# Normalised tokens turned by DRAM and VectorE instead of TensorE, in the MLP half of an adaLN block (pairs 1 to 7)

## The chip, the cores and the metric

One core of a Trainium2 chip. The metric is device time in microseconds (us) of one execution of the whole kernel. The engines are called by their names in the profile: PE (TensorE matmuls, with PEld for its weight loads), DVE (VectorE), ACT (ScalarE), POOL (GpSimd) and SP (SyncE, which here only issues DMAs). All data is float32; matmuls run on float32r operands, each split into a high and a low part and multiplied in three terms.

## The reference

An adaptive-layernorm transformer block: an attention half and then an MLP half. S = 2048 tokens, D = 640 features, F = 1728 hidden features. The half that matters here:

```python
mod = (_silu(c) @ w_mod).reshape(c.shape[0], 6, 1, -1)
sa, ca, ga, sb, cb, gb = (mod[:, 0], mod[:, 1], mod[:, 2], mod[:, 3], mod[:, 4], mod[:, 5])
...
x = x + ga * _A_ref(h, A_wqkv, A_w_phi, A_wo)
h = _layernorm(x, axis=-1) * (1 + cb) + sb
x = x + gb * _B_ref(h, B_w1, B_b1, B_w2, B_b2)
# _B_ref: h = relu(x @ w1 + b1) ** 2 ; out = h @ w2 + b2
```

## The kernel before

**Tiles.** The 2048 tokens are 8 pairs of 2 x 128 tokens (`NB` = 8 pairs, j = 0 to 7). The 640 features are `NC` = 5 chunks of 128, the hidden features 14 blocks (`NF`, the last one 64 wide) taken two at a time: `NP` = 7 double blocks, n = 0 to 6.

**A step.** The MLP runs pair by pair; each pair takes 14 steps, and in step `at` = 2n or 2n + 1 PE does `up(j, at)`, which multiplies chunk by chunk W1's block with the pair's normalised and transposed tokens `H2[j]` (15 matmuls of 256 columns: five chunks, three terms each, 10 in step 13), and then `down(0)` or `down(1)`, one half of W2's product for the double block before. What `up` leaves in PSUM goes ACT relu (L1255), DVE square (L1256), then ACT copy to the high part `ra` (L1279) and DVE subtraction to the low part (L88); pairs from `PLAIN` = 2 on also form four sums on DVE (L1270) and split those into `rs` (L1295 on ACT, L88 on DVE). `down` multiplies `ra` and `rs` with W2's rows, which lie in SBUF or, from pair 2 on, come from DRAM through a ring of four buffers (`ring_a`, `ring_b`, `ring_c`, issued by POOL).

**The next pair's input.** While pair j runs, `layer(j + 1, at)` does the work for the next pair, by a table per pair (`LN_AT0` for pair 1, `LN_AT1` for 2, `LN_AT2` for 3, `LN_AT` for 4 to 7) that names the step of each piece: "load" and "xx" fetch attention's result `XM` and the residual `XX`, "add" adds them on DVE (L1079) and stores the sum, "ln" gives the steps of six ACT passes (two sums L1503, two sums of squares L1508, two scalings L1515, one for each tile of 128 tokens; small POOL instructions L1505 and L1510 to L1512 stand between them), and the entries with a number call `t2` for the chunks named. `t2` transposes two tiles of one or two chunks on PE (`t_in`, L357, a matmul with the identity, into a PSUM bank) and turns them into `H2` (`t_out`: ACT scale and shift L368 with the condition's columns `cols_b`, ACT copy to the high part L369, DVE subtraction to the low part L88). `XX` serves as scratch for `t_out`. Pair 0's input is made in the attention half.

**What sets the order.** In the MLP the order on PE, DVE, ACT and POOL is the order in which the code emits the instructions (`manual_schedule`), and SP's too, but for pair 1, where a scheduler places its DMAs. Each engine works its own list in order, so an instruction that waits holds all that stand behind it. On ACT and DVE a step's own work stands first, and `layer`'s pieces of that step behind it.

Of the kernel before, what the change touches and what calls it, by code (L numbers as in the profile page):

```python
# [8 lines left out]
F32 = mybir.dt.float32  # L9
# [12 lines left out]
NT = S // P  # L22
NC = D // P
# [28 lines left out]
def kernel(  # L52
# [19 lines left out]
    nc = tc.nc  # L72
# [14 lines left out]
    def lo(out_lo, full, hi, eng=None):  # L87
        (eng or nc.vector).tensor_tensor(out_lo, full, hi.bitcast(F32), op=ALU.subtract)  # L88
# [8 lines left out]
    dram = ctx.enter_context(tc.tile_pool(name="dram", bufs=1, space=bass.MemoryType.DRAM))  # L97
# [19 lines left out]
    def row(tag, name):  # L117
        return (pc if tag in ("s3", "s4") else mem).tile([P, D], F32, tag=tag, name=name, bufs=BUFS[tag])
# [19 lines left out]
    def tp(name):  # L138
        return psA.tile([P, 512], F32, tag="tp", name=name)
# [20 lines left out]
    ident = const.tile([P, P], F32, name="ident")  # L160
# [10 lines left out]
    cols_b = const.tile([P, 10], F32, name="cols_b")  # L171
# [145 lines left out]
    MA = {}  # L317
# [34 lines left out]
        for _ in ln_parts(xt, nm, spare):  # L352
            pass

    def t_in(xn, d, p):
        for i in range(2):
            nc.tensor.transpose(p[:, i * P : (i + 1) * P], xn[:, i, d * P : (d + 1) * P], ident)  # L357

    def t_unit(xn, cols, hT, d, nm, p=None):
        if p is None:  # L360
            p = tp(f"t{nm}_{d}")
        t_in(xn, d, p)
        t_out(cols, hT, d, nm, p)

    def t_out(cols, hT, d, nm, p, hf=None):
        if hf is None:
            hf = row("s3", f"hf{nm}_{d}")[:, :256]
        nc.scalar.activation(hf, p[:, :256], AF.Identity, bias=cols[:, d : d + 1], scale=cols[:, 5 + d : 6 + d])  # L368
        nc.scalar.activation(hT[:, d, 0], hf, AF.Copy)  # L369
        lo(hT[:, d, 1], hf, hT[:, d, 0])  # L370
# [12 lines left out]
    def t1(j, *ds, more=None):  # L383
        if 0 in ds:
            HT[j] = ht(f"hT{j}", j)
        p = tp(f"ta{j}_{ds[0]}")
        for k, d in enumerate(ds):
            t_in(XB[j], d, p[:, 256 * k : 256 * k + 256])
        if more:
            mod_turn(more[0], p[:, 256:], 4)  # L390
        for k, d in enumerate(ds):
            t_out(cols_a, HT[j], d, f"a{j}", p[:, 256 * k : 256 * k + 256])
        DONE[:] = newest(ET_.Activation), newest(ET_.DVE)
        if more:
# [318 lines left out]
    for t in range(2, NT - 2):  # L713
        j, i = divmod(t, 2)
# [12 lines left out]
        p = proj("v", t, (1, 0, lambda: t1(j + 1, 4)) if t == NT - 3 else None)  # L727
# [76 lines left out]
    def bank(nm):  # L804
        return psB.tile([P, 512], F32, tag="m", name=nm)
# [226 lines left out]
    todo = {"load": list(preps), "hi": list(preps), "lo": list(preps)}  # L1032
# [29 lines left out]
    def load_xm(j):  # L1062
        XM[j] = tok2("x0", f"xm{j}")
        for i in range(2):
            nc.sync.dma_start(XM[j][:, i], A1[2 * j + i])

    def load_xx(j):
        if j:
            XX[j] = [row("s2" if j <= PLAIN else "s1", f"xx{j}_{i}") for i in range(2)]
        else:  # L1070
            both = tok2("x1", "xx0")
            XX[j] = [both[:, i] for i in range(2)]
        for i in range(2):
            t = 2 * j + i
            nc.sync.dma_start(XX[j][i], x[t * P : (t + 1) * P])
# [6 lines left out]
    def t2(j, *ds):  # L1082
        if 0 in ds:
            H2[j] = ht(f"h2_{j}", j, (0, 96))
        if j == 0:
            t_unit(XM[j], cols_b, H2[j], ds[0], f"b{j}", bank(f"tb{j}_{ds[0]}"))
            return
        p = tp(f"tb{j}_{ds[0]}")
        for k, d in enumerate(ds):
            t_in(XM[j], d, p[:, 256 * k : 256 * k + 256])  # L1090
        for k, d in enumerate(ds):
            t_out(cols_b, H2[j], d, f"b{j}", p[:, 256 * k : 256 * k + 256], XX[j][d % 2][:, :256])

    NB = NT // 2
    places += [new(f"w{w}") for w in W_AT[-23:-19] + W_AT[-18:-16] + W_AT[-15:]] + [new(tag) for tag in ("k", "k", "q0", "q1")]
# [393 lines left out]
    prev = None  # L1489
    LN2 = {}  # L1490

    LN_AT0 = {"load": 2, "xx": 3, "add": (5, 6), "ln": (5, 6, 7, 7, 8, 9), 10: (0, 1), 11: (2, 3), 12: (4,)}
    LN_AT1 = {"load": 3, "add": (5, 5), "ln": (5, 6, 6, 7, 8, 8), 9: (0, 1), 11: (2, 3), 12: (4,)}
    LN_AT2 = {"load": 0, "xx": 3, "add": (6, 6), "ln": (7, 7, 8, 8, 9, 9), 10: (0, 1), 11: (2, 3), 12: (4,)}
    LN_AT = {"load": 0, "add": (3, 4), "ln": (4, 5, 6, 6, 7, 7), 8: (0, 1), 10: (2, 3), 12: (4,)}
    PREPS = iter([1, 3] + [2, 1, 2, 2, 1, 2] + [1, 1] + [1, 2])

    def ln_pieces(xt, nm, spare):
# [204 lines left out]
```

## Time and profile before

| what | value |
|---|---|
| median of 3 runs (lowest, highest) | 766.42 us (765.6, 767.21) |
| the profiled execution's own time | 766.05 us |
| its span, first to last instruction | 764.3 us |
| busy: PE / DVE / ACT / POOL | 758.5 / 593.9 / 435.6 / 144.9 us |
| granted TensorE clock | 1.000 |
| DMA moved | 126.69 MB, mean 166 GB/s |
| MLP half | from 387.7 us to the end; a pair takes about 46 us |

A time in the traces counts from the span's start. A row of a timeline gives start, length, engine, line, operation, output and inputs, and how many instructions were merged; in brackets stands how long the engine sat idle before and who released it. Instructions on an engine overlap a little, so the pace is read from start to start.

### The profile page before, as it was taken

How to read it: one execution, taken by the hardware profiler on the slowest of the kernel's cores; microseconds unless marked ns; L12 is line 12 of the kernel's file. 1: busy time of each engine (PE TensorE's matmuls, PEld its weight loads, DVE VectorE, ACT ScalarE, POOL GpSimd, SP SyncE). 2: the span in 40 equal slices, each digit the busy share in tenths (PEclk: the TensorE clock that was granted, in tenths of full speed). 3: DMA queues.
4: the chain of work that ended last, by engine and by line, in shares of the span. 5: the costliest groups of instructions: out<-in, count | busy, mean ns of one | idle time of the engine just before them, and what ended most of it. 6: DMA issues, size and time to landing. Idle time of an engine off the chain costs nothing.

```text
span 764.3 us, 15303 instructions
## 1 busy us (share of the span) xinstructions
PE 758.5 (99%) x5968; PEld 739.7 (97%) x5968; DVE 593.9 (78%) x1083; ACT 435.6 (57%) x972; POOL 144.9 (19%) x301
## 2 busy tenths in 40 slices
PE   9999999999999999999999999999999999999997
PEld 8999999999999989988999999999999999999997
DVE  6598897988999899999655667876767666685666
ACT  5766756677853364546776647465563645536331
POOL 3001101001100255432101000231321313213110
PEclk9999999999999999999999999999999999999999
DMA  8811431343332345223366466996766759767460
GB/s 322 329 61 78 138 104 54 104 136 112 126 104 93 109 150 188 72 87 104 122 194 221 120 227 236 283 334 209 224 166 207 232 179 268 199 184 204 126 184 35
DMA packets 51505, 126.69 MB, mean 166 GB/s; under 512 B 6684, under 2 KB 7457, under 8 KB 51433
## 3 DMA queue, kind: packets, MB, share of 16 engines
q1 hardware_dynamic: 34098, 84.65, 32.8%
q0 software_dynamic: 14752, 35.76, 16.9%
q10 hardware_dynamic: 2583, 5.30, 1.8%
q8 instruction: 47, 0.77, 0.5%
q14 instruction: 25, 0.20, 0.1%
HBM read 95.70 MB, written 29.89 MB: 164 GB/s over the span
## 4 chain that ended last, share of the span: by engine, by line
PE 91%; DVE 7%; DMA 1%; issue 0%; SPq 0%; ACT 0%; DVEq 0%
PE up L78 24%; PE acc L78 18%; PE pq L78 9%; PE pk L78 9%; PE pv L78 9%; PE pwo L78 6%; PE acc3x L78 5%; PE kvp L450 3%; PE te L920 1%; DVE dn L878 1%; DVE scr L876 1%; DVE ezb L900 1%; PE tb L357 1%; PE ta L357 1%; DVE ot L88 1%; PE foldq L280 1%
## 5 line engine op out<-in xcount | busy, mean ns | idle before, releaser
L78 PE MATMUL up<-h,w 128*128 128x256 f32 x1640 | 206.4, 278 | 0.0
L78 PEld LDWEIGHTS up<-h,w 128*128 128x128 f32 x1640 | 196.1, 188 | 0.0
L1255 ACT ACTIVATE ft<-up,b_t 128x256 f32<-128x256 f32 x104 | 49.1, 472 | 113.8 <-PE up L78 113.2
L78 PE MATMUL acc<-w,ra 128*128 128x384 f32 x452 | 97.4, 335 | 0.0
L1256 DVE TENSOR_TENSOR ft<-ft 128x256 f32<-128x256 f32 x104 | 44.1, 424 | 48.4 <-ACT ft L1255 46.8
L78 PE MATMUL pwo<-wo,ot 128*128 128x256 f32 (+3 forms) x512 | 80.5, 312 | 0.1
L78 PEld LDWEIGHTS pwo<-wo,ot 128*128 128x128 f32 (+1 forms) x512 | 74.4, 188 | 3.2 <-issue 2.7
L78 PE MATMUL pq<-wq,hT 128*128 128x384 f32 (+1 forms) x480 | 75.2, 312 | 0.0
L78 PEld LDWEIGHTS acc<-w,ra 128*128 128x128 f32 x452 | 72.7, 188 | 0.8 <-DVE ra L88 0.5
L78 PE MATMUL pk<-wk,hT 128*128 128x384 f32 (+1 forms) x480 | 72.7, 308 | 0.0
L78 PE MATMUL pv<-wv,hT 128*128 128x384 f32 (+1 forms) x480 | 71.7, 307 | 0.0
L78 PEld LDWEIGHTS pq<-wq,hT 128*128 128x128 f32 x480 | 71.1, 188 | 0.6 <-issue 0.2
L78 PEld LDWEIGHTS pk<-wk,hT 128*128 128x128 f32 x480 | 70.5, 188 | 0.4 <-issue 0.2
L78 PEld LDWEIGHTS pv<-wv,hT 128*128 128x128 f32 x480 | 70.1, 188 | 0.0
L88 DVE TENSOR_TENSOR ra<-ft,ra 128x384 fp32r<-128x384 f32 (+2 forms) x86 | 36.8, 449 | 32.6 <-ACT ra L1279 19.3
L1365 POOL DMA_DIRECT2D ring_a<-td_a x34 | 18.3, 539 | 126.1 <-PE acc L78 100.4
L1279 ACT ACTIVATE ra<-ft 128x384 fp32r<-128x384 f32 x48 | 25.2, 526 | 28.4 <-DVE ft L1256 22.4
L78 PE MATMUL acc3x<-w,ra 128*128 128x256 f32 x231 | 39.8, 278 | 0.0
L78 PEld LDWEIGHTS acc3x<-w,ra 128*128 128x128 f32 x231 | 37.2, 188 | 0.2 <-DVE ra L88 0.2
L1270 DVE TENSOR_TENSOR ft<-ft 128x128 f32<-128x128 f32 x136 | 33.4, 287 | 1.2
L441 DVE TENSOR_REDUCE sk<-ek 128x64 f32<-128x1280 f32 x16 | 23.7, 1484 | 12.4 <-ACT ek L436 10.8
L884 POOL TENSOR_TENSOR dn<-dn,rs_q 128x32 f32<-128x32 f32 x32 | 20.2, 630 | 66.7 <-DVE dn L878 66.4
(270 smaller groups left out, 1412.6 us busy)
## 6 DMA issues: line engine op xcount, KB each, us to landing
ring_c<-td_c POOLq DMA_DIRECT2D x34, 384.0 KB, 4.2
ring_a<-td_a POOLq DMA_DIRECT2D x34, 384.0 KB, 4.1
ring_b<-td_b POOLq DMA_DIRECT2D x34, 256.0 KB, 4.0
esp<-eq SPq DMA_DIRECT2D x12, 640.0 KB, 3.0
el<-esp SPq DMA_DIRECT2D x12, 640.0 KB, 3.9
rw<-in_w SPq DMA_DIRECT2D x23, 320.0 KB, 2.9
wm<-in_w_mod SPq DMA_DIRECT2D x20, 320.0 KB, 3.3
xb<-in_x SPq DMA_DIRECT2D x8, 640.0 KB, 4.2
```

The costliest lines, as they stand in the source:

```text
L78: nc.tensor.matmul(o, a, b, start=first and i == 0, stop=last and i == len(terms) - 1, skip_group_check=skip,)
L88: (eng or nc.vector).tensor_tensor(out_lo, full, hi.bitcast(F32), op=ALU.subtract)
L280: nc.tensor.matmul(p[g // 3][:, (g % 3) * 120 : (g % 3) * 120 + n], r, bd_t[:120, g * 120 : g * 120 + n], start=True, stop=True,)
L357: nc.tensor.transpose(p[:, i * P : (i + 1) * P], xn[:, i, d * P : (d + 1) * P], ident)
L441: nc.vector.tensor_reduce(s, heads(flat(e)), axis=AX.X, op=ALU.add)
L450: nc.tensor.matmul(kvp[g // 4][64 * c : 64 * c + 64, a : a + 2 * n].rearrange("p (s n) -> p s n", s=2), v[:, u], e[:, :, o : o + n], start ...
L884: nc.gpsimd.tensor_tensor(dn[:, s], dn[:, s], rs[:, 1 - s], op=ALU.mult)
L1255: nc.scalar.activation(r, p, AF.Relu, bias=b1_t[:, f : f + 1])
L1256: nc.vector.tensor_tensor(r, r, r, op=ALU.mult)
L1270: nc.vector.tensor_tensor(t[:, o], t[:, a], t[:, b], op=op)
L1279: nc.scalar.activation(a[:, 0, :3], t[:, :3], AF.Copy)
L1365: nc.gpsimd.dma_start(RING[j, n, r], TD[n][r].bitcast(F32R))
```

## The change

For pairs 1 to 7 the PE transposes are taken out. In their place, after a pair's second scaling, `deal(j)` writes the normalised tokens with four DMAs to a DRAM buffer `XN`, one DMA for each 32 partitions, and `dealt(j)` reads them back with two DMAs into `XX`, so that partition 32q + t then holds, of the tokens 32a + t, the q-th quarter of the features. `turn(j)` transposes blocks of 32 x 32 on DVE (two instructions, one for each tile, each of 640 columns) from `XX` into `XM`. Feature 5p + b then lies on partition p in chunk b; W1's rows (on the host) and the condition's shift and scale columns (`mod_turn` for parts 3 and 4) are put in the same order, and pair 0's PE transposes read their columns with a step of five. `t_out` takes its input from `XM` in SBUF and writes its scaled result in place. `XM` thus stays in use until the last `t_out`. The tables move: the six ACT passes come earlier or closer together, `turn` is in step 10, `dealt` in step 9, and `t_out` in steps 11, 12 and 13 (chunks 0 and 1, 2 and 3, and 4).

```diff
@@ mod_turn
-            nc.tensor.transpose(p[:, i * P : (i + 1) * P], MA[part][:, c * P : (c + 1) * P], ident)
+            src = by_turn(MA[part])[:, c] if part in (3, 4) else MA[part][:, c * P : (c + 1) * P]
+            nc.tensor.transpose(p[:, i * P : (i + 1) * P], src, ident)
...
+    def by_turn(ap):
+        return ap.rearrange("p (f b) -> p b f", b=NC)
@@ t2
-        p = tp(f"tb{j}_{ds[0]}")
-        for k, d in enumerate(ds):
-            t_in(XM[j], d, p[:, 256 * k : 256 * k + 256])
-        for k, d in enumerate(ds):
-            t_out(cols_b, H2[j], d, f"b{j}", p[:, 256 * k : 256 * k + 256], XX[j][d % 2][:, :256])
+        for d in ds:
+            hf = XM[j].rearrange("p s d -> p (s d)")[:, 256 * d : 256 * d + 256]
+            t_out(cols_b, H2[j], d, f"b{j}", hf, hf)
+
+    XN = [dram.tile([4, 2, P, D // 4], F32, name=f"xn{j}") for j in range(NT // 2)]
+
+    def deal(j):
+        for a in range(4):
+            nc.sync.dma_start(
+                XN[j][a].rearrange("i (q t) c -> t i q c", q=4),
+                XM[j][32 * a : 32 * a + 32].rearrange("t i (q c) -> t i q c", q=4),
+            )
+
+    def dealt(j):
+        for i in range(2):
+            nc.sync.dma_start(XX[j][i].rearrange("p (a c) -> p a c", a=4), XN[j][:, i].rearrange("a p c -> p a c"))
+
+    def turn(j):
+        xt = XM[j].rearrange("p s d -> p (s d)").rearrange("p (b i a t) -> p i a b t", b=NC, i=2, t=32)
+        for i in range(2):
+            nc.vector.transpose(xt[:, i], XX[j][i].rearrange("p (a t b) -> p a b t", a=4, t=32))
...
-    LN_AT = {"load": 0, "add": (3, 4), "ln": (4, 5, 6, 6, 7, 7), 8: (0, 1), 10: (2, 3), 12: (4,)}
+    TURNED = {"turn": 10, 11: (0, 1), 12: (2, 3), 13: (4,)}
+    LN_AT = {"load": 0, "add": (3, 4), "ln": (4, 5, 5, 6, 6, 7), **TURNED}
@@ layer
                 next(LN2[j])
+                if i == 5:
+                    deal(j)
+        if todo["turn"] == at + 1:
+            dealt(j)
+        if todo["turn"] == at:
+            turn(j)
```

The moves on the engines are shown for pair 3, which prepares pair 4 (`h_4`). Lines of the changed kernel are numbered 5 to 22 higher: L368 and L369 of `t_out` are L373 and L374 there, the relu L1255 and L1259 are L1276 and L1280, the copies L1279 and L1289 are L1300 and L1310, L1508 and L1515 are L1530 and L1537.

First, ACT in steps 6 and 7, where the passes of the layer norm stand among the step's own work (`sqb`, `nbb` are the small columns that POOL makes between the squares and the scalings). Before:

```order
L1255 ACTIVATE ft_3_6899<-up,b_t 128x2x128
L1295 ACTIVATE rs_2_6902<-ft_2_6816 128x512
L1508 ACTIVATE xx_0_6668,sqb_6836<-xm_6665,smb_6835 128x640
L1508 ACTIVATE xx_1_6669,sqb_6836<-xm_6665,smb_6835 128x640
L1255 ACTIVATE ft_3_6899<-up,b_t 128x256
L1279 ACTIVATE ra_3_6942<-ft_3_6899 128x384
L1515 ACTIVATE xm_6665<-xm_6665,nbb_6837,sqb_6836 128x640 x2
```

And in the changed kernel:

```order
L1530 ACTIVATE xx_0_6661,sqb_6829<-xm_6658,smb_6828 128x640
L1276 ACTIVATE ft_3_6893<-up,b_t 128x2x128
L1316 ACTIVATE rs_2_6896<-ft_2_6809 128x512
L1530 ACTIVATE xx_1_6662,sqb_6829<-xm_6658,smb_6828 128x640
L1537 ACTIVATE xm_6658<-xm_6658,nbb_6830,sqb_6829 128x640
L1276 ACTIVATE ft_3_6893<-up,b_t 128x256
L1300 ACTIVATE ra_3_6936<-ft_3_6893 128x384
L1537 ACTIVATE xm_6658<-xm_6658,nbb_6830,sqb_6829 128x640
```

The first square has moved ahead of step 6's relu, and the first scaling from behind step 7's `ra` copy to directly behind the second square, ahead of step 7's relu.

Second, DVE in steps 10 and 11 (`xr` is the residual that gets its bias, `ft_5` the hidden block that is squared). Before:

```order
L88 TENSOR_TENSOR rs_4_7069<-ft_4_6982,rs_4_7069 128x512
L1424 TENSOR_TENSOR xr_3_0_6921<-xr_3_0_6921,bb 128x640
L1424 TENSOR_TENSOR xr_3_1_6923<-xr_3_1_6923,bb 128x640
L88 TENSOR_TENSOR h_4_6999<-xx_0_6668,h_4_6999 128x256
L88 TENSOR_TENSOR h_4_6999<-xx_1_6669,h_4_6999 128x256
L1256 TENSOR_TENSOR ft_5_7066<-ft_5_7066 128x256
L88 TENSOR_TENSOR ra_5_7113<-ft_5_7066,ra_5_7113 128x384
```

And in the changed kernel:

```order
L88 TENSOR_TENSOR rs_4_7056<-ft_4_6979,rs_4_7056 128x512
L1445 TENSOR_TENSOR xr_3_0_6915<-xr_3_0_6915,bb 128x640
L1445 TENSOR_TENSOR xr_3_1_6917<-xr_3_1_6917,bb 128x640
L1113 STREAM_TRANSPOSE xm_6658<-xx_0_6661 128x4x5x32
L1113 STREAM_TRANSPOSE xm_6658<-xx_1_6662 128x4x5x32
L1277 TENSOR_TENSOR ft_5_7053<-ft_5_7053 128x256
L88 TENSOR_TENSOR ra_5_7091<-ft_5_7053,ra_5_7091 128x384
```

The two transposes stand where two of the five low parts of `h_4` stood, ahead of step 11's square.

Third, ACT in the last two steps of the pair. Before:

```order
L1255 ACTIVATE ft_6_7151<-up,b_t 128x2x128
L1295 ACTIVATE rs_5_7154<-ft_5_7066 128x512
L368 ACTIVATE xx_0_6668<-tb_4_7168,cols_b 128x256
L369 ACTIVATE h_4_6999<-xx_0_6668 128x256
L1259 ACTIVATE ft_6_7151<-up,b_t 64x256
L1282 ACTIVATE ra_6_7187<-ft_6_7151 128x128
L1285 ACTIVATE ra_6_7187<-ft_6_7151 128x128
L1289 ACTIVATE ra_6_7187<-ft_6_7151 64x256
```

And in the changed kernel, where the two `t_out` of step 11 (L373 and L374, twice) stand directly ahead of these rows:

```order
L1276 ACTIVATE ft_6_7136<-up,b_t 128x2x128
L1316 ACTIVATE rs_5_7139<-ft_5_7053 128x512
L373 ACTIVATE xm_6658<-xm_6658,cols_b 128x256
L374 ACTIVATE h_4_7114<-xm_6658 128x256
L373 ACTIVATE xm_6658<-xm_6658,cols_b 128x256
L374 ACTIVATE h_4_7114<-xm_6658 128x256
L1280 ACTIVATE ft_6_7136<-up,b_t 64x256
L1303 ACTIVATE ra_6_7172<-ft_6_7136 128x128
L1306 ACTIVATE ra_6_7172<-ft_6_7136 128x128
L1310 ACTIVATE ra_6_7172<-ft_6_7136 64x256
L373 ACTIVATE xm_6658<-xm_6658,cols_b 128x256
L374 ACTIVATE h_4_7114<-xm_6658 128x256
```

All five `t_out` now lie in the last three steps, and the fifth has moved from ahead of step 13's relu (L1259) to behind that step's last copy.

More of the change, by code (lines that the diff above doesn't have):

```diff
@@ L353, in layer_norm, with t_in @@
             pass
-    def t_in(xn, d, p):
+    def by_turn(ap):
+        return ap.rearrange("p (f b) -> p b f", b=NC)
+    def t_in(xn, d, p, mixed=False):
         for i in range(2):
-            nc.tensor.transpose(p[:, i * P : (i + 1) * P], xn[:, i, d * P : (d + 1) * P], ident)
+            src = by_turn(xn[:, i])[:, d] if mixed else xn[:, i, d * P : (d + 1) * P]
+            nc.tensor.transpose(p[:, i * P : (i + 1) * P], src, ident)
     def t_unit(xn, cols, hT, d, nm, p=None):
@@ L361, in t_unit @@
             p = tp(f"t{nm}_{d}")
-        t_in(xn, d, p)
+        t_in(xn, d, p, True)
         t_out(cols, hT, d, nm, p)
@@ L1490 @@
     LN2 = {}
-    LN_AT0 = {"load": 2, "xx": 3, "add": (5, 6), "ln": (5, 6, 7, 7, 8, 9), 10: (0, 1), 11: (2, 3), 12: (4,)}
-    LN_AT1 = {"load": 3, "add": (5, 5), "ln": (5, 6, 6, 7, 8, 8), 9: (0, 1), 11: (2, 3), 12: (4,)}
-    LN_AT2 = {"load": 0, "xx": 3, "add": (6, 6), "ln": (7, 7, 8, 8, 9, 9), 10: (0, 1), 11: (2, 3), 12: (4,)}
-    LN_AT = {"load": 0, "add": (3, 4), "ln": (4, 5, 6, 6, 7, 7), 8: (0, 1), 10: (2, 3), 12: (4,)}
+    TURNED = {"turn": 10, 11: (0, 1), 12: (2, 3), 13: (4,)}
+    LN_AT0 = {"load": 1, "xx": 2, "add": (4, 5), "ln": (4, 5, 6, 6, 7, 7), **TURNED}
+    LN_AT1 = {"load": 3, "add": (5, 5), "ln": (5, 5, 6, 6, 7, 7), **TURNED}
+    LN_AT2 = {"load": 0, "xx": 3, "add": (5, 5), "ln": (5, 5, 6, 6, 7, 7), **TURNED}
+    LN_AT = {"load": 0, "add": (3, 4), "ln": (4, 5, 5, 6, 6, 7), **TURNED}
     PREPS = iter([1, 3] + [2, 1, 2, 2, 1, 2] + [1, 1] + [1, 2])
@@ L1672 @@
     w1 = [B_w1[:, f * P : f * P + n] for f, n in enumerate(FS)]
-    w1 = np.stack([np.tile(w, (1, P // w.shape[1])).reshape(NC, P, P).transpose(1, 0, 2) for w in w1])
+    w1 = np.stack([np.tile(w, (1, P // w.shape[1])).reshape(P, NC, P) for w in w1])
     w_ss = w_mod[:, : 2 * D].reshape(NC, P, 2, NC, P).transpose(3, 1, 0, 2, 4).reshape(NC * P, 2 * D)
```

## The prediction

> **What bounds the kernel now.** The page comes first: busy times, then the shares of the chain that ended last.
>
> ```profile
> PE 758.5 (99%) x5968; PEld 739.7 (97%) x5968; DVE 593.9 (78%) x1083; ACT 435.6 (57%) x972; POOL 144.9 (19%) x301
> PE 91%; DVE 7%; DMA 1%; issue 0%; SPq 0%; ACT 0%; DVEq 0%
> ```
>
> PE is busy without a gap, so a microsecond taken from PE is a microsecond of the kernel, as long as ACT, DVE and the DMAs hand over their part as early as PE then asks for it. How much slack there is, is read from the timelines of one pair. Pair 3, which prepares pair 4, starts at 527.7 us. PE's, from step 6 on:
>
> ```profile
> 546.92 1.86 PE L78 MATMUL up<-h,w 128*128 128x256 f32 x15
> ...
> 553.42 1.86 PE L78 MATMUL up<-h,w 128*128 128x256 f32 x15
> 555.12 1.20 PE L78 MATMUL acc<-w,ra 128*128 128x384 f32 x6
> ...
> 556.68 0.60 PE L357 MATMUL tb<-ident,xm 128*128 128x128 f32 x4
> 557.04 2.01 PE L78 MATMUL up<-h,w 128*128 128x256 f32 x15
> ...
> 560.45 1.86 PE L78 MATMUL up<-h,w 128*128 128x256 f32 x15
> ...
> 567.41 1.86 PE L78 MATMUL up<-h,w 128*128 128x256 f32 x15
> ...
> 570.67 0.38 PE L357 MATMUL tb<-ident,xm 128*128 128x128 f32 x2
> 570.80 1.43 PE L78 MATMUL up<-h,w 128*128 128x256 f32 x10
> 572.07 0.69 PE L78 MATMUL acc<-ring_a,rs 128*128 128x384 f32 x3
> ...
> 573.63 1.86 PE L78 MATMUL up<-h,w 128*128 128x256 f32 x15
> ```
>
> No idle time stands at any row. `up` takes 1.70 us (553.42 to 555.12), so 0.113 a matmul; `down` takes 1.56 (555.12 to 556.68), nine matmuls at 0.17. A step of two tiles without transposes is 546.92 to 553.42 = 6.50 us, with four of them 553.42 to 560.45 = 7.03.
>
> **What goes: the PE transposes.** Four cost 7.03 - 6.50 = 0.53; the next four 567.41 - 560.45 - 6.50 = 0.46; the last two 0.27 (0.13 until `up` starts, and ten matmuls in 1.27 where 1.13 is their pace). That is 1.26 us a pair, 8.8 us in seven pairs, and all of it is on the path. With nothing late, that would be the result.
>
> **What is late next: ACT, from the layer norm to the pair's end.** ACT, POOL and DVE in the same pair:
>
> ```profile
> 550.59 0.82 ACT L1508 ACTIVATE xx<-xm,smb 128x640 f32<-128x640 f32 x1
> ...
> 552.08 0.48 ACT L1255 ACTIVATE ft<-up,b_t 128x256 f32<-128x256 f32 x1 [0.58 <-PE up L78]
> 553.05 0.53 ACT L1279 ACTIVATE ra<-ft 128x384 fp32r<-128x384 f32 x1 [0.49 <-DVE ft L1256]
> 553.48 1.72 ACT L1515 ACTIVATE xm<-xm,nbb,sqb 128x640 f32<-128x640 f32 x2
> ...
> 564.35 0.57 ACT L368 ACTIVATE xx<-tb,cols_b 128x256 f32<-128x256 f32 x1 [1.01 <-PE tb L357]
> 564.95 0.42 ACT L369 ACTIVATE h<-xx 128x256 fp32r<-128x256 f32 x1
> 565.28 0.55 ACT L368 ACTIVATE xx<-tb,cols_b 128x256 f32<-128x256 f32 x1
> ...
> 569.31 0.48 ACT L1255 ACTIVATE ft<-up,b_t 128x256 f32<-128x256 f32 x1 [1.65 <-PE up L78]
> 569.68 0.62 ACT L1295 ACTIVATE rs<-ft 128x512 fp32r<-128x512 f32 x1
> ...
> 572.27 0.47 ACT L1259 ACTIVATE ft<-up,b_t 64x256 f32<-64x256 f32 x1 [0.16 <-PE up L78]
> ...
> 573.67 0.42 ACT L1289 ACTIVATE ra<-ft 64x256 fp32r<-64x256 f32 x1 [0.40 <-DVE ft L1261]
> ```
> ```profile
> 551.60 0.18 POOL L1510 TENSOR_SCALAR sqb<-sqb 128x2 f32<-128x2 f32 x1 [0.27 <-ACT xx L1508]
> ...
> 552.66 0.41 POOL L1512 TENSOR_TENSOR nbb<-smb,sqb 128x2 f32<-128x2 f32 x1
> ```
> ```profile
> 553.61 0.56 DVE L88 TENSOR_TENSOR ra<-ft,ra 128x384 fp32r<-128x384 f32 x1 [0.59 <-PE acc L78]
> ...
> 563.98 1.56 DVE L1424 TENSOR_TENSOR xr<-xr,bb 128x640 f32<-128x640 f32 x2
> ...
> 572.13 0.42 DVE L88 TENSOR_TENSOR h<-xx,h 128x256 fp32r<-128x256 f32 x1 [1.11 <-ACT h L369]
> ```
>
> *Steps 6 to 8.* The first scaling now stands between the second square and step 7's relu, and it needs POOL's columns, 1.5 us after the squares (551.60 to 552.66 + 0.41). By the pieces ahead of it the second square starts 0.3 earlier, at 550.3; the columns are there at 552.9, and the relu follows one scaling (0.81) later, at 553.76 instead of 552.08. From relu to high part is 553.05 + 0.53 - 552.08 = 1.50, to low part 2.09: 555.26 and 555.85. PE asks for the first at 555.12, for the second two matmuls on. It waits about 0.4 us, where nothing waited before. The second scaling ends at 556.1, not at 555.2.
>
> *Steps 10 to 12.* DVE has its bias additions behind it at 565.35 (row 563.98, shifted by -0.53 + 0.4, plus two paces of 0.74). The two block transposes have no row. The nearest by size and form:
>
> ```profile
> L430 DVE TENSOR_REDUCE mxk<-k 128x32 f32<-128x640 f32 x16 | 12.9, 809 | 0.0
> L441 DVE TENSOR_REDUCE sk<-ek 128x64 f32<-128x1280 f32 x16 | 23.7, 1484 | 12.4 <-ACT ek L436 10.8 <-ACT ek L437 1.3
> ```
>
> One source of 640 columns takes 0.81, which I take; as a bound I take twice the columns, 1.48. Below 0.81 would gain at most 0.3 a pair. So the turn ends at 566.9 if its data is there. Behind it on DVE wait the square of `ft_5`, the low part `ra_5` and the sums: the high part is ready at 567.9, the low one at 568.5. PE wants them at 568.5 and 568.9. The cover is 0.4 us; each further microsecond is PE's.
>
> *The pair's end.* ACT is then never free: `ra` copy from 567.36 (0.44 pace), two `t_out` (0.93 each, from 564.35 to 565.28; L369 follows L368 after 0.60 and its start is 0.33 from the next), relu 0.37, `rs` 0.53, two `t_out` 1.86, so step 13's relu starts at 572.42. From it to the last copy 573.67 - 572.27 = 1.40 goes by, since DVE's two instructions lie between; 0.33 on, the fifth `t_out` starts at 574.15, its high part ends at 575.2, its low part at 575.6. PE: step 12 starts at 567.41 - 0.53 - 0.46 + 0.4 = 566.8; 3.26, ten matmuls of step 13 (1.13), 1.56 of `down`, and twelve matmuls of the next pair's first `up` (1.36) bring it to the fifth chunk at 574.15. It waits about 1.4 us. Before, that low part was ready at 572.55 and not needed before 575.1. Even with ACT free all the time a wait stays: 1.60 (last copy after the end of `up`, 572.07 to 573.67) + 0.33 + 0.60 + 0.45 + 0.43 = 3.4 until the low part against 1.56 + 1.36 + 0.11 = 3.0 of PE, so 0.4 us.
>
> **The way through DRAM.** The DMAs' times to landing:
>
> ```profile
> xm<-a SPq DMA_DIRECT2D x16, 320.0 KB, 4.4
> xx<-in_x SPq DMA_DIRECT2D x16, 320.0 KB, 5.0
> x<-xm SPq DMA_DIRECT2D x16, 320.0 KB, 3.0
> ```
> ```profile
> q1 hardware_dynamic: 34098, 84.65, 32.8%
> ```
>
> The first three move rows of 2,560 bytes, 128 to a transfer; the new ones move the same 640 KB each way in pieces of 640 bytes, 1,024 to a passage instead of 256. No row has such pieces. By bytes, the four writes go from 556.1, 0.35 apart, and land by 560.2 (3.0); the reads, which SP holds back until all four have landed, land at 564.7 to 565.3, the second 0.4 later. Against 565.35 and 566.1 on DVE that is 0 to 0.2 late. By pieces, each at the mean of SP's queue (0.328 x 16 x 764.3 / 34,098 = 0.118 us), the 768 more would take 768 x 0.118 / 16 = 5.7 us more a passage; that is the other end. I take 0.2 a passage, near the bytes, as the writes' pieces can be carried while the next is issued: 0.5 us late with the 0.1 from above, and all of it reaches the pair's end. A gain over whole rows I exclude. The added 9.2 MB are otherwise costed at nothing, since the ring of four buffers covers its fetches.
>
> So for each of pairs 4 to 7: -1.26 + 0.4 + 0.5 + 1.4 = +1.04 us, in all +4.2.
>
> **Pairs 1 to 3.** Pair 3 has no wait in steps 6 to 8 (both squares and both scalings stand together), but its bias additions (1.5 us) lie in step 12, ahead of DVE's last steps: an end of 1.5, net +0.3. In pairs 1 and 2 the reads stand on SP behind loads of W2:
>
> ```profile
> 411.53 8.64 SPq L1006 DMA_DIRECT2D rw<-in_w  x4
> ```
> ```profile
> 468.36 1.42 SPq L1319 DMA_DIRECT2D traw<-in_w  x2
> ```
>
> For pair 1 they cannot issue before 420.2 (411.53 + 8.64), land by 425.0, and the turn ends 3 us after the 422.7 at which DVE is free for it. PE's step has room for that, the chain to the end has not, and the bias additions lie in it: PE reaches the fifth chunk at 433.5, the chunk comes at about 437: net -1.26 + 3.7 = +2.4. For pair 2 the reads follow the first of the two loads, at 468.9, and land by 473.7, 3.5 after DVE is free; behind the turn stand four subtractions of the W2 split as well. `ra_5` comes 2.3 late, and 1.4 is lost at the end: +2.4.
>
> Two more edits are taken at nothing. `XM` is free only behind the last `t_out`, 4 us later, but its next sum is wanted 14 us on (steps 3 and 4). The 20 transposes on PE that now read with a step of five (pair 0 and the condition's parts) cost between nothing and twice their weight load, 20 x 0.14 = 2.8 us:
>
> ```profile
> L357 PEld LDWEIGHTS tb<-ident,xm x80: 137/140/143, 381.7 to 708.6; 128*128 128x128 f32 x80
> ```
>
> **Sum.** 4.2 + 0.3 + 2.4 + 2.4 = +9.3: 766.05 + 9.3 = 775.4 for an execution like the profiled one, which lies 0.37 below the median: 776.
>
> **The rivals.** *Faster: only the floor is lost.* The reads are early, the relu is not held, and each end costs 0.4: -0.86 a pair, -6.0, 760.4 by the median. For it: every one of my waits is a difference of chains some 8 us long, and 0.2 us in each link decides. Against: the relu's delay and the end are in the order itself.
>
> *Slower still: the pieces are late.* Halfway to the price by pieces the two passages take 5.7 us more a pair, and 40 us are lost; a quarter of the way, 2.8 more in each of seven pairs, gives 776 + 7 x 2.4 (0.4 is in the forecast) = 793, which I take. Against it: no transfer of SP's above, writes or reads, lands later than 5.0.
>
> *Slower: the block transpose takes twice its columns,* 1.48: 2 x 0.67 = 1.35 more in the chain of each pair, 9.4 in all: 785. Its source steps by five elements, 20 bytes, and no row has such a step. [...]
>
> **Chances.** Forecast, with its own range 768 to 783: 0.46; floor only: 0.20; late pieces: 0.19; slow transpose: 0.15. A measurement of this kernel can tell 0.2%, 1.5 us. The faster rival lies below 764.9 nearly whole, the low tail of the forecast holds no change: faster 0.19, same 0.08, slower 0.73. The range 761 to 794 leaves out the far half of the late pieces and nearly half of the faster rival, some 0.18.
>
> **What would show it.** Right: 14 transposes of about 0.8 us; PE's weight load of `up` waiting for the low part `h` some 1 to 2 us at each pair's start; a step 7 relu 1.5 us late behind a scaling that waits for POOL; transposes that wait for their DMA in pairs 1 and 2 and hardly later. Wrong: PE without gaps at the pair boundaries (then the 8.8 us come through), transposes waiting for DMA by over a microsecond in pairs 4 to 7, or lasting 1.4 us.

## The result: 800.8 us, 4.5% slower, and the profile after

| | before | changed |
|---|---|---|
| median (lowest, highest) of 4 runs each | 766.82 us (765.6, 767.39) | 800.78 us (799.82, 802.95) |
| ratio, 95% interval | | 1.045 [1.0431, 1.0469] |
| span of the profiled execution | 764.3 us | 798.3 us |
| mean granted TensorE clock | 1.000 | 0.994 |

Times here and below are medians over executions; one execution of the spaced kernel below ran at a granted clock of 0.754, took 937 us and is left out.

The forecast was 776, range 761 to 794: the direction was right, the size was not. Of the 34 us lost, and of the 8.8 that PE's transposes should have given, the changed kernel's page shows this: PE's share of the span, the chain that ended last, and SP's queue.

```profile
PE 768.2 (96%) x5898; PEld 740.0 (93%) x5898; DVE 611.5 (77%) x1097; ACT 435.7 (55%) x972; POOL 142.6 (18%) x301
PE 62%; DVE 16%; ACT 8%; DMA 6%; issue 3%; POOL 2%; SPq 1%; DVEq 0%; ACTq 0%; POOLq 0%
...
q1 hardware_dynamic: 49106, 93.83, 35.4%
```

The 70 matmuls are gone (5,968 to 5,898), yet PE is busy for 9.7 us longer, and the chain, once PE for 91%, now runs through DVE, ACT and DMAs for 30%. What PE waited for is best read from its weight loads, whose rows show more of a wait than the matmuls' own: 12.0 us for `ra` (L1300) where those show 10.4. The waits of PEld in the changed kernel; columns are the total, the number of waits and the longest:

```profile
PEld acc L78 <- ACT ra L1300: 12.0, 8, 4.1
PEld up L78 <- ACT ft L1276: 7.9, 10, 2.9
PEld up L78 <- ACT h L374: 5.2, 6, 3.3
PEld up L78 <- DVE ft L1281: 3.3, 5, 1.0
PEld acc L78 <- DVE ra L88: 2.9, 10, 0.3
...
PEld up L78 <- DVE h L88: 1.9, 7, 0.3
PEld acc L78 <- DMA ring_b<-td_b: 1.8, 1, 1.8
```

These seven make 35.0 us; of all these kinds the kernel before had 0.5 us, for `DVE ra`. A second part is the clock: 0.006 of 798.3 is 4.8 us. Together that is most of the 34.0 + 8.8 = 42.8.

Where in the pairs it lies, from the start of one pair's step 13 to the next one's (us; the column of pair 1 ends with the start of pair 1's step 13):

| | pair 1 | pair 2 | pair 3 | pair 4 | pair 5 | pair 6 |
|---|---|---|---|---|---|---|
| before | 48.16 | 46.27 | 45.93 | 46.02 | 45.93 | 46.01 |
| changed | 57.46 | 56.35 | 48.66 | 48.89 | 48.84 | 49.33 |

Pairs 1 and 2 lose 9.3 and 10.1 us, the pairs behind them 2.7 to 3.3 each; 1.35 more are lost ahead of these columns, in pair 0, and 1.5 behind them.

**A steady pair.** PE's timeline of pair 4, from pair 3's step 13 (594.26) to its own (643.15):

```profile
594.26 1.42 PE L78 MATMUL up<-h,w 128*128 128x256 f32 x10 [0.17 <-ACT ft L1276]
...
597.61 1.68 PE L78 MATMUL up<-h,w 128*128 128x256 f32 x12 [0.38 <-DVE ft L1281]
599.45 0.96 PE L78 MATMUL up<-h,w 128*128 128x256 f32 x3 [0.16 <-ACT h L374]
...
601.71 1.93 PE L78 MATMUL up<-h,w 128*128 128x256 f32 x15
...
625.05 1.99 PE L78 MATMUL up<-h,w 128*128 128x256 f32 x15 [0.44 <-ACT ft L1276]
...
640.90 1.56 PE L78 MATMUL acc<-w,ra 128*128 128x384 f32 x6 [0.87 <-ACT ra L1300]
...
643.15 1.42 PE L78 MATMUL up<-h,w 128*128 128x256 f32 x10 [0.17 <-ACT ft L1276]
```

The idle times in the brackets sum to 2.0 us from 597.61 on, but four stops cost 4.05 by the starts: from step 13 to the next pair's second `up` 601.71 - 594.26 = 7.45 where it was 5.96 (570.80 to 576.76), 0.14 of that for transposes, step 7 3.85 for 3.25 (621.20 to 625.05) and 0.1 behind it, step 12 4.98 for 3.26 (638.17 to 643.15). 4.05 - 1.26 = 2.8, of the 2.87 by which this period is longer. The brackets show less than the stop because a modelled matmul ends some 0.16 after its successor starts (the row of an undisturbed `up` is 1.86 long, and the next row starts after 1.70), and because a merged row shows only the wait before its first matmul. The weight loads of the same place show the wait inside it, for the low part:

```profile
599.45 0.19 PEld L78 LDWEIGHTS up<-h,w 128*128 128x128 f32 x1 [0.36 <-ACT h L374]
599.90 0.30 PEld L78 LDWEIGHTS up<-h,w 128*128 128x128 f32 x2 [0.27 <-DVE h L88]
```

What DVE does in steps 10 to 12 of that pair (the residual's bias, the two block transposes, the square of step 11, the low part that PE asks for):

```profile
635.27 1.55 DVE L1445 TENSOR_TENSOR xr<-xr,bb 128x640 f32<-128x640 f32 x2
637.38 2.60 DVE L1113 STREAM_TRANSPOSE xm<-xx 128x640 f32<-128x640 f32 x2 [0.56 <-DMA xx<-xn]
639.91 0.38 DVE L1277 TENSOR_TENSOR ft<-ft 128x256 f32<-128x256 f32 x1
640.88 0.56 DVE L88 TENSOR_TENSOR ra<-ft,ra 128x384 fp32r<-128x384 f32 x1 [0.59 <-ACT ra L1300]
```

The two transposes take 2.6 us, and the square of step 11, whose relu started at 636.84, comes behind them at 639.91. PE's wait of 0.87 hangs on it.

**Pairs 1 and 2.** Their largest stops on PE, and what DVE or ACT sat waiting for ahead of those at 486.53, 543.35 and 523.05:

```profile
439.39 1.10 PE L78 MATMUL up<-h,w 128*128 128x256 f32 x3 [3.13 <-ACT h L374]
...
486.53 1.04 PE L78 MATMUL acc<-w,ra 128*128 128x384 f32 x3 [3.92 <-ACT ra L1300]
...
505.52 0.76 PE L78 MATMUL acc<-ring_a,rs 128*128 128x384 f32 x3 [0.68 <-DVE y L1445]
...
508.59 1.01 PE L78 MATMUL acc<-ring_b,rs 128*128 128x256 f32 x3 [1.60 <-DMA ring_b<-td_b]
...
523.05 1.99 PE L78 MATMUL up<-h,w 128*128 128x256 f32 x15 [2.61 <-ACT ft L1276]
...
543.35 1.56 PE L78 MATMUL acc<-w,ra 128*128 128x384 f32 x6 [2.07 <-ACT ra L1300]
```
```profile
481.46 2.55 DVE L1113 STREAM_TRANSPOSE xm<-xx 128x640 f32<-128x640 f32 x2 [4.66 <-DMA traw<-in_w]
...
539.88 2.56 DVE L1113 STREAM_TRANSPOSE xm<-xx 128x640 f32<-128x640 f32 x2 [3.27 <-DMA xx<-xn]
```
```profile
521.08 0.74 ACT L1525 ACTIVATE xx<-xm 128x640 f32<-128x640 f32 x1 [2.46 <-DVE xm L1084]
```

In pairs 1 and 2 the transposes wait 4.66 and 3.27 us and hold the square behind them. The first of these rows names the W2 load that stands on SP right behind the reads (issued at 477.27); what the transposes take in is the reads' data, issued at 476.12. In step 3 of pair 2 the stops of 0.68 and 1.60 us, with the granted clock at 0.50 behind the second (508.59 to 510.59; see the last section), cost 4.3 by the starts, since steps 3 and 4 take 10.81 for 6.50. In pair 2, moreover, both sums of the layer norm now stand ahead of step 6's relu and wait 2.46 for DVE's additions, which stand behind DVE's W2 work.

### The profile page after: what moved, and what is told of

Its sections match the earlier page's. It is cut to its first block, busy times and chain, and to the rows that moved or that the text cites. A ratio compares the mean times of both kernels' runs of the same rounds, so it can differ in the third digit from the quotient of the medians.

```text
span 798.3 us, 15235 instructions
## 1 busy us (share of the span) xinstructions
PE 768.2 (96%) x5898; PEld 740.0 (93%) x5898; DVE 611.5 (77%) x1097; ACT 435.7 (55%) x972; POOL 142.6 (18%) x301
## 4 chain that ended last, share of the span: by engine, by line
PE 62%; DVE 16%; ACT 8%; DMA 6%; issue 3%; POOL 2%; SPq 1%; DVEq 0%; ACTq 0%; POOLq 0%
PE up L78 13%; PE acc L78 10%; PE pk L78 9%; PE pv L78 9%; PE pq L78 7%; PE pwo L78 4%; PE acc3x L78 3%; DMA xx<-xn 3%; PE kvp L455 2%; DVE dn L883 2%; DMA xn<-xm 2%; DVE scr L881 2%; DVE ezb L905 2%; ACT xm L373 2%; ACT h L374 2%
## 5 line engine op out<-in xcount | busy, mean ns | idle before, releaser
L78 PE MATMUL up<-h,w 128*128 128x256 f32 x1640 | 212.2, 281 | 12.1 <-ACT ft L1276 5.2
L78 PEld LDWEIGHTS up<-h,w 128*128 128x128 f32 x1640 | 200.2, 190 | 18.4 <-ACT ft L1276 7.9
L1276 ACT ACTIVATE ft<-up,b_t 128x256 f32<-128x256 f32 x104 | 48.8, 470 | 130.1 <-PE up L78 130.0
L78 PE MATMUL acc<-w,ra 128*128 128x384 f32 x452 | 101.5, 342 | 10.4 <-ACT ra L1300 10.4
L1300 ACT ACTIVATE ra<-ft 128x384 fp32r<-128x384 f32 x48 | 25.2, 525 | 49.8 <-DVE ft L1277 43.7
```

Source lines behind the costliest of these rows:

```text
L78: nc.tensor.matmul(o, a, b, start=first and i == 0, stop=last and i == len(terms) - 1, skip_group_check=skip,)
L1276: nc.scalar.activation(r, p, AF.Relu, bias=b1_t[:, f : f + 1])
L1300: nc.scalar.activation(a[:, 0, :3], t[:, :3], AF.Copy)
```

## The experiments

Four kernels first take the change apart.

**Only pairs 4 to 7 turned** (`t2` transposes on PE for j < 4, with the old tables):

```diff
+        if j < 4:
+            p = tp(f"tb{j}_{ds[0]}")
+            ...  t_in(XM[j], d, ..., True); t_out(..., XX[j][d % 2][:, :256])
+            return
-    LN_AT0 / LN_AT1 / LN_AT2 of the change
+    LN_AT0 / LN_AT1 / LN_AT2 of the kernel before
```

> Only pairs 4 to 7 are turned through DRAM; pairs 1 to 3 keep PE's transposes (read with a step of five) and the steps of the kernel before. Theory 'two stages': the steady pairs lose some 2.9 us each by themselves (their period was 48.9 us instead of 46.0), and pairs 1 to 3 lose what is left, by what stands around their turn on SP, ACT and DVE. Then this kernel takes 766.8 + 4 x 2.9 = 778 us, up to 780 with the strided transposes, and PE has no wait over 1 us before pair 3. Rival 'spread': the loss comes from something that the whole program shares (the new order of the features, the added DRAM traffic, PE's clock), and pairs 1 to 3 stay slow without the turn: 790 us or more.

Measured: 779.06 us, ratio 1.0158 [1.0138, 1.0179]. Periods of pairs 4 to 6 are 49.0, 49.7 and 49.3, of pairs 1 and 2 48.3 and 47.7. The steady loss belongs to the turned pairs themselves, and the other 22 us of the changed kernel to the turn of pairs 1 to 3 with the tables that go with it. One sign of the theory failed: PE waits 1.18 us for `ring_b` in pair 2.

**Contiguous transposes:**

```diff
-  nc.vector.transpose(xt[:, i], XX[j][i].rearrange("p (a t b) -> p a b t", a=4, t=32))
+  nc.vector.transpose(xt[:, i], XX[j][i].rearrange("p (a b t) -> p a b t", a=4, t=32))
```

> The block transposes read 32 columns that lie side by side, not 20 bytes apart (the features come out in another order than W1's rows, so the output is another one; the instructions and sizes are the same). Theory 'stride': they then take about 0.8 us instead of 1.35, the wait of PE for the ra copy in step 12 goes from 0.87 us to under 0.3, and each of the seven pairs gets some 1.1 us back: 793 us. Rival 'no stride': they stay at 1.3 us, since the time is the instruction's own, and the kernel stays at 800 to 801.

Measured: 794.18 us, 1.0353 [1.0318, 1.0387]. The group rows of the transposes (count, busy us, mean ns, idle before), of the changed kernel and of this one:

```profile
L1113 DVE STREAM_TRANSPOSE xm<-xx 128x640 f32<-128x640 f32 x14 | 18.2, 1335 | 11.2 <-DMA xx<-xn 5.5 <-DMA traw<-in_w 4.7 <-issue 1.0
```
```profile
L1113 DVE STREAM_TRANSPOSE xm<-xx 128x640 f32<-128x640 f32 x14 | 11.8, 845 | 13.5 <-DMA xx<-xn 12.3 <-issue 1.1
```

The step of 20 bytes makes 845 ns into 1,335, and that is worth 6.6 us where 7.8 were expected; the four executions lie between 790.4 and 797.2. DVE then waits more for the data (13.5 for 11.2), and PE's stop in step 12 of pair 4 shrinks without going: that step takes 4.14 us, where it took 4.98 and undisturbed takes 3.26.

**No passage; then no transposes either.**

```diff
-                if i == 5:
-                    deal(j)
-        if todo["turn"] == at + 1:
-            dealt(j)
```
```diff
-        if todo["turn"] == at:
-            turn(j)
```

> The passage through DRAM is left out: no deal, no dealt, and the transposes read what the squares left in XX (so the output is another one). Theory 'two stages': pairs 4 to 7 get back only the 0.56 us that their turn waited, since the slow transposes and the late fifth chunk stay; pairs 1 and 2 get back the waits that came from SP (3.9 and 2.1 us in step 12, 1.6 for the ring, and the slower clock behind them), 8 to 14 us in all: 784 to 791. Rival 'passage': the passage is what costs everywhere, and without it the kernel is at 768 or below.

> Passage and transposes are left out, only the new tables stay: t_out reads the scaled tokens where they are (so the output is another one), and PE transposes nothing. Theory 'order': the relu behind the scaling (0.7 us in step 8) and the fifth chunk behind step 13's relu (about 0.4 to 1.4 us at the pair's end) stay, so that a steady pair is at 46.0 - 1.26 + 1.1 to 2.1, and pair 1's late sums (2.6 us in pair 2's step 7) stay too: 767 to 775 us. Rival 'turn only': without the turn nothing is late and the whole 8.8 us come through: 758 us.

Measured: 786.38 us, 1.0253 [1.0235, 1.027], without the passage; 775.92 us, 1.012 [1.0102, 1.0138], without the transposes as well. The first came out as its first theory had it. So did the second in kind (its steady pairs take 46.4 us, and 45.8 to 46.8 were expected), though its time lies 0.9 above that theory's range; it is still slower than the kernel before, though in pairs 1 to 7 PE has no transposes to do. Then the passes:

**Only t_out late** (the kernel without passage and transposes, with additions and passes of all pairs in the old steps):

```diff
-    LN_AT = {"load": 0, "add": (3, 4), "ln": (4, 5, 5, 6, 6, 7), **TURNED}
+    LN_AT = {"load": 0, "add": (3, 4), "ln": (4, 5, 6, 6, 7, 7), **TURNED}
... (the other three tables likewise)
```

> The kernel without passage and transposes (775.9 us, so the output is another one), with the additions and the six passes of all pairs back in the steps of the kernel before; only the steps of t_out (11, 12, 13) are the changed kernel's. Theory 'two parts of the order': the 2.6 us in front of pair 2's step 8, with the slower clock behind them, and the 0.45 us in step 8 of the pairs behind it go; the late t_out stays with 0.8 to 1 us a pair: 766 to 769. Rival 'late t_out only': the place of the passes costs nothing that t_out would not cost anyway: 774 to 776.

Measured: 768.55 us, 1.0033 [1.0021, 1.0044]. PE's timeline at the start of its pair 5 (the first `up` in twelve and three matmuls, and the second `up`):

```profile
621.59 1.52 PE L78 MATMUL up<-h,w 128*128 128x256 f32 x12
623.30 0.96 PE L78 MATMUL up<-h,w 128*128 128x256 f32 x3 [0.19 <-ACT h L374]
...
625.57 1.93 PE L78 MATMUL up<-h,w 128*128 128x256 f32 x15
```

With nothing else late, the fifth chunk alone makes this step 3.98 us instead of 3.13, for a bracket of 0.19. So the whole loss can be laid out, each line being what went when one more thing was left out, in this order (t_out's line against the kernel before without its transposes, 766.8 - 8.8 = 758.0, which is worked out, not run). The first column goes by the medians, the others by the profiled executions. Another order could share the loss out otherwise, and the line of t_out's steps also holds whatever else the change leaves in that kernel, such as PE's strided transposes:

| left out | whole, us | pairs 0 to 2, to step 13 of pair 2 | each of pairs 3 to 6 |
|---|---|---|---|
| the passage through DRAM | 14.4 | 10.9 | 0.76 |
| the transposes on DVE | 10.5 | 1.7 | 1.78 |
| the passes' new steps | 7.4 | 5.6 | 0.71 |
| t_out's new steps | 10.5 | 6.3 | 0.97 |
| PE's transposes gained | -8.8 | -3.8 | -1.26 |

**Relu order.** The first of three attempts to mend pairs 4 to 7 puts their passes back:

```diff
-    LN_AT = {..., "ln": (4, 5, 5, 6, 6, 7), **TURNED}
+    LN_AT = {..., "ln": (4, 5, 6, 6, 7, 7), **TURNED}
```

> The kernel in which only pairs 4 to 7 are turned (779.1 us), with the six passes of these pairs back in the steps of the kernel before (4, 5, 6, 6, 7, 7): both squares and no scaling stand ahead of step 7's relu, both scalings behind step 7's ra copy. Theory 'relu held': the wait of 0.45 us in front of step 8's up goes, with PE's slow restart behind it some 0.7 us a pair, so 776.3 us. Rival 'later deal': the second scaling ends later than it did, the turn and the ra copy of step 12 come later by the same, and nothing is gained: 778 to 780.

Measured: 780.54 us, 1.0187 [1.0166, 1.0209]: nothing is gained, as the rival said (and half a microsecond above its range), but not for its reason. Step 8's wait is gone, but PE's waits for `ra` in step 12 are 1.73, 2.42, 1.98 and 1.34 us where they were 0.87 to 1.82. Counted from the start of PE's step 8, the deals are issued when they were, 1.8 us on. But the reads now follow the first deal by 6.9 to 7.5 us, where that was 5.4 to 6.7: part of what was won is lost again in the passage. Why it takes longer is not shown.

**Early.**

```diff
+    LN_AT = {"load": 0, "add": (2, 3), "ln": (3, 4, 4, 4, 5, 5), "turn": 9, 10: (0, 1), 11: (2, 3), 12: (4,)}
-                if n == 5 + (j == PLAIN) - (j == NB - 1):   # the residual's bias
+                if n == 4 + 2 * (j == PLAIN):
```

> The kernel in which only pairs 4 to 7 are turned (779.1 us), with their preparation a step or two earlier: sums of x in steps 2 and 3, the six passes in steps 3, 4, 4, 4, 5 and 5, the turn in step 9, t_out in steps 10, 11 and 12, and the residual's bias in step 8. Theory 'place': passage, slow transposes and t_out are all hidden then, PE loses nothing and the 1.26 us of its transposes come through in each of the four pairs: 766.8 + 1 (what pairs 1 to 3 cost in that kernel) - 5 = 763 us, 761 to 765, below the kernel before. Rival 'length': two transposes of 1.35 us don't fit beside DVE's own work of steps 9 and 10 wherever they stand, the squares and low parts behind them come late, and PE waits 0.5 to 1 us a pair: 766 to 770.

Measured: 785.75 us, 1.0251 [1.0234, 1.0268]. Neither theory: the pair's end no longer waits, but other things are late. SP's queue and DVE in pair 4, and the stretches of 4 us (the last two columns are the DMA engines' busy share and GB/s):

```profile
603.10 2.97 SPq L1108 DMA_DIRECT2D xn<-xm  x4
606.11 1.89 SPq L1442 DMA_DIRECT2D xr<-x  x2
613.22 0.94 SPq L1115 DMA_DIRECT2D xx<-xn  x2
```
```profile
613.91 0.83 DVE L1452 TENSOR_TENSOR xr<-xr,bb 128x640 f32<-128x640 f32 x1 [4.25 <-DMA xr<-x]
```
```profile
602.00:606.00 4.00, 4.00 (x34) 4.00 (x33) 2.05 (x4) 1.82 (x5) 1.00 (x2) 1.00 1.05 294
606.00:610.00 4.00, 4.00 (x33) 4.00 (x32) 2.58 (x7) 1.14 (x3) 0.78 (x3) 1.00 1.06 304
610.00:614.00 4.00, 4.00 (x36) 4.00 (x36) 0.09 (x1) 0.48 (x1) 1.41 (x3) 1.00 0.99 338
```

The reads can be issued only 7 us after the last deal, and the residual behind the deals lands so late that DVE waits 4.25 us for it (16.5 in all), with the squares behind; PE's waits for `ra` and `rs` come to 13.2 us. The mean busy share of the 16 DMA engines is 0.99 to 1.06 in each of these stretches.

**Spaced, and the same without passage.** The residual goes ahead of the deals (n = 2), the passes stand between the two versions, turn and t_out as in the change, and the residual's bias as in the early kernel:

```diff
+    LN_AT = {"load": 0, "add": (2, 3), "ln": (4, 4, 5, 5, 6, 6), **TURNED}
-            if n == (5, 5, 5, 3)[min(j, 3)]:   # residual(j)
+            if n == (5, 5, 5, 2)[min(j, 3)]:
```

> The kernel in which only pairs 4 to 7 are turned (779.1 us), with their sums of x in steps 2 and 3, the six passes in steps 4, 4, 5, 5, 6 and 6, turn and t_out where the change has them (10, and 11 to 13), and the residual fetched a step pair earlier, ahead of the deals instead of behind them, with its bias in step 8, away from the turn. Theory 'spacing': what made the early kernel slow were transfers that crowded each other; with the residual ahead of the deals the passage lands some 11 us after the second scaling, just as DVE is free in step 10, and only the pair's end costs 0.4 to 0.9: 763 to 765 us. Rival 'full engines': the 16 DMA engines have no room for the passage beside the ring's fetches wherever it stands, deals and reads land late again, DVE is held by over a microsecond in each pair and what waits behind it with it: 770 to 785.

> The same kernel without deals and reads (the transposes read what the squares left, so the output is another one). Theory 'spacing': nearly nothing changes, 762 to 764 us, since the passage was hidden; the slow transposes fit into DVE's gap in step 10. Rival 'full engines': the kernel is 8 us or more faster than with the passage. Third, 'length': also without passage PE waits 0.5 to 1 us for the ra copy in step 12 of each pair, and the kernel stays at 766 to 768.

Measured: 775.76 us, 1.0113 [1.0093, 1.0133], and without the passage 766.89 us, 1.0007 [0.9997, 1.0016]. DVE in step 10 of pair 4 with the passage:

```profile
615.09 1.38 DVE L1120 STREAM_TRANSPOSE xm<-xx 128x640 f32<-128x640 f32 x1 [1.45 <-DMA xx<-xn]
616.87 1.35 DVE L1120 STREAM_TRANSPOSE xm<-xx 128x640 f32<-128x640 f32 x1 [0.41 <-DMA xx<-xn]
```

The scalings ended at 602.4; the first tile is there 12.7 us later and the second 14.5, where the changed kernel's pair 4 had its first after 10.5 (626.83 to 637.38). The passage costs these four pairs 8.9 us, which speaks for full engines. Without it no wait for `ra` is left in step 12, so the slow transposes do fit into DVE's gap ("length" falls); but the pairs last 45.97 us, exactly as before: the fifth chunk's end eats the whole 1.26.

**Whole rows.** The last question on the passage is whether its pieces or its bytes cost:

```diff
-                XN[j][a].rearrange("i (q t) c -> t i q c", q=4),
-                XM[j][32 * a : 32 * a + 32].rearrange("t i (q c) -> t i q c", q=4),
+                XN[j][:, 32 * a : 32 * a + 32].rearrange("i t d -> t i d"),
+                XM[j][32 * a : 32 * a + 32],
...
-            nc.sync.dma_start(XX[j][i].rearrange("p (a c) -> p a c", a=4), XN[j][:, i].rearrange("a p c -> p a c"))
+            nc.sync.dma_start(XX[j][i], XN[j][i])
```

> The changed kernel, all seven pairs turned, but the passage moves whole rows: the same four writes and two reads of the same bytes, in pieces of 2,560 bytes instead of 640 (partitions get whole tokens back, so the output is another one). Theory 'bytes': the passage costs what its bytes cost on DMA engines that are nearly full already; the kernel stays within 2 us of 800.8. Rival 'pieces': the four times as many pieces make it late; with rows the reads land 1 to 3 us earlier, the waits of DVE's transposes and of PE in step 12 go, and the kernel comes to 788 to 795, towards the 786.4 us without a passage.

Measured: 797.53 us, 1.0409 [1.0383, 1.0434]: 3.3 us less than with pieces of 640 bytes, just between the two theories. Issues (KB each, median us to landing) of the changed kernel and of this one:

```profile
xn<-xm SPq DMA_DIRECT2D x28, 160.0 KB, 3.0
xx<-xn SPq DMA_DIRECT2D x14, 320.0 KB, 4.6
```
```profile
xn<-xm SPq DMA_DIRECT2D x28, 160.0 KB, 3.1
xx<-xn SPq DMA_DIRECT2D x14, 320.0 KB, 4.8
```

A quarter of the 14.4 us goes with the pieces, and not through the median landing times. By the traces 2.8 of the 3.3 are there at step 13 of pair 2: the reads, which wait until all four deals have landed, follow the first deal 37.4 us later in the sum of the seven passages, where it was 42.5, most of all in pair 2 (5.2 for 7.4), and PE's stop of 2.07 us there is gone. The steady pairs gain nothing (48.9 us each in both kernels).

**Two steps of t_out earlier** (residual and bias as in the spaced kernel):

```diff
+    LN_AT = {"load": 0, "add": (2, 3), "ln": (3, 4, 4, 4, 5, 5), "turn": 10, 11: (0, 1, 2), 12: (3, 4)}
```

> An attempt to pass the kernel before, correct in its output: pairs 4 to 7 turned, sums in steps 2 and 3, passes in steps 3, 4, 4, 4, 5 and 5, the residual ahead of the deals with its bias in step 8, the turn in step 10, and t_out in steps 11 (chunks 0 to 2) and 12 (3 and 4), so that nothing of it stands behind step 13's relu. If the passage lands in the 13 us that it now has, the pair's end costs nothing and the 1.26 us come through: 762 to 764 us. Rival 'full engines': the passage takes longer the earlier it starts, since the ring, the stores and the residual share the engines with it; DVE waits 1 to 3 us in step 10 and the kernel is at 768 to 778.

Measured: 777.39 us, 1.0136 [1.0102, 1.017], inside the rival's range. The turn waits for its reads (7.5 us in six waits), and three t_outs in step 11 hold step 12's relu, for which step 13's `up` waits 1.11 us in each pair. None of the versions with a turn that were tried passes the kernel before.

## Why the prediction was wrong, step by step

- **PE's transposes, -1.26 a pair: right.** Steps 10 and 11 of pair 4, 7.02 before, take 6.50 without them, as assumed (631.67 to 638.17).
- **The relu behind the scaling, +0.4: right in place, small in size.** The bracket is 0.44, but step 7 took 0.6 more and 0.1 stood behind; 0.71 by the runs. Its wait was for the PSUM slot that the relu frees, not for the high part.
- **The transposes, 0.81 each: the step that failed in the steady pairs.** I took the row of 640 contiguous columns and gave the strided case, the third rival, 0.15. The instruction takes 1.335; contiguous it takes 0.845, so the row was good for the form that the kernel doesn't use. The transposes cost 1.78 us a pair, since the square and the copy of step 11 wait behind them; in my sum the turn left that chain 0.4 us of cover.
- **The passage, 0.2 late: right on the landing, wrong on the rest.** Medians of 3.0 and 4.6 are the times for whole rows that I used, and the "late pieces" rival is false as a price by pieces (5.7 us a passage; measured 3.3 us for all seven). But my sum followed one transfer through an idle machine. In the steady pairs the passage costs 0.76; in pairs 1 and 2 it costs most of its 14.4 us.
- **The pair's end, +1.4: right.** 1.63 by the starts against a pace without transposes: 0.97 for the fifth chunk, as worked out, and 0.66 ahead of it for `ft` (the late relu of step 13), which the sum did not name. The floor that I gave if nothing else is late, 0.4, was too low: 0.85 with only t_out late, 1.28 in the spaced kernel without passage.
- **The preparation of pairs 1 to 3, +2.4, +2.4 and +0.3: the step that failed by most.** At step 13 of pair 2 the changed kernel is 20.7 us behind (545.60 against 524.87) where my sum has at most 5.1; that is 16 of the 25 us by which the forecast fell short. 6.7 of the 20.7 are there by step 2 of pair 1 and 5.2 more by step 2 of pair 2, where the sum had 2.4 each; 8.9 come in steps 2 to 12 of pair 2, where it had 0.3. Pair 1's wait was right: PE stands 3.13 us for the fifth chunk, 3.7 predicted. For pair 2 the copy of step 11 was to come 2.3 late; the wait was 3.92, because DVE waited 4.66 for the reads where 3.5 were expected, and the two transposes took 2.55 where 1.62 were. For pair 3, "no wait in steps 6 to 8" was read from the squares and scalings alone: the two sums ahead of them wait for DVE's additions and hold a relu (2.61), and the turn waits for its reads too (2.07). Not in the sum at all were the clock (below; some 1.7 us three times), pair 0, which lost 1.35 with waits of 0.41 and 0.95 us for `ra`, and a stop for `ring_b` (1.60). The last stands with 0.35 to 1.31 us also in five of the six kernels in which pairs 1 to 3 are not turned, with 1.31 in one that has no deals at all, so the deals are not its whole cause, and that stays open.
- **Taken at nothing.** The 20 strided transposes on PE load their weights in 0.20 us instead of 0.14, 1.2 us at most: inside the bound. The ring's cover did not hold in pair 2, where PE stopped 1.60 us for `ring_b`.

The rivals "slow transpose" (785) and "late pieces" (793) each had one true part; the result lay outside the range because the terms of pairs 1 to 3 were differences of single chains, with no bound of their own.

## What to carry to other kernels

To take work off the bounding engine did not pay here, since what replaced it did not fit the other queues: 1.26 us of PE bought a chain of 10 to 15 us through SP, full DMA engines, DVE and ACT, and four places where PE then stopped. Price an instruction by a row with its own access pattern, and follow the moved pieces through each differently built stage (the first pairs here) rather than through the steady one alone. Read stops from start to start and from the weight loads: in a steady pair the idle time in brackets showed half of what they cost.

## What the runs showed of the hardware

- **After some short stops the granted clock fell.** Stretches of 4 us behind the first two stops of the list under "Pairs 1 and 2", and before them (the eighth column is the granted clock):

```profile
436.00:440.00 4.00, 0.79 (x4) 0.39 (x4) 3.17 (x8) 1.61 (x5) 0.00 (x0) 1.00 0.00 0
440.00:444.00 4.00, 4.00 (x19) 4.00 (x20) 1.23 (x3) 0.47 (x1) 0.00 (x0) 0.57 0.52 164
484.00:488.00 4.00, 1.47 (x8) 1.17 (x9) 3.03 (x9) 2.01 (x5) 0.00 (x0) 0.98 0.70 258
488.00:492.00 4.00, 4.00 (x21) 4.00 (x20) 3.14 (x10) 3.17 (x8) 0.65 (x1) 0.59 0.75 241
```

  In the trace the granted clock stands at 0.50 for 3.41 us each time (from 440.06 and from 487.85 here), so the stop of 3.13 us cost some 1.7 more (an estimate, half of 3.41). It also fell at the stop of 1.60 (0.57 from 508 to 512, with a stop of 0.68 three us before) and, in the relu-order kernel, after 1.73 and 1.98 us (0.50 from 572.90 to 574.90 and from 671.81 to 673.81), but not after 2.42 in that same kernel (1.00 from 620.66 to 626.66); it stayed at 1.00 after 2.61 in the changed kernel's pair 2 (523.05 to 529.05) and fell to 0.59 after the same 2.61 in the kernel without turn:

```profile
512.00:516.00 4.00, 4.00 (x22) 4.00 (x21) 1.17 (x3) 2.22 (x6) 1.57 (x4) 0.59 1.02 295
```

  So equal stops ended differently; what decides it is not shown.
- **A step of five elements** cost DVE's block transpose 1.58 times the time (1,335 against 845 ns), and PE's weight load 1.4 times (0.20 against 0.14 us, medians of the transposes that write `tb`).
- **The DMA engines were full in stretches that the mean hides.** The mean of the changed kernel is 170 GB/s, but in the stretch of a pair in which the ring runs they are busy at 0.99 to 1.06 and 290 to 340 GB/s (early kernel, 602 to 614 us), and in the kernel before, without a passage, at 1.03 to 1.05 (593.6 to 601.6). 1.3 MB more there landed not in 3.0 + 4.6 us but up to 14.5 after the data was ready, and the median deal landed after 4.2 us in the spaced kernel and 5.6 in the early one.
